# Linear attention and a two-layer FFN on one core: one batch's divisions and x transposition moved ahead of the next batches' loads, and the last group's PSUM tile and stores split

## The chip, the core and the metric

The kernel runs on one core of a Trainium2 chip. The metric is device time in microseconds (us) of one launch. The core has a matrix engine (PE; its weight loads are listed as PEld), a vector engine (DVE), an activation engine (ACT), a general engine (POOL) and an engine that here only issues transfers (SP). Each works through its own instructions strictly in order and waits on semaphores. Transfers are issued from the SP queue, a few from the ACT queue, and are carried out by 16 DMA engines. PE writes its results to PSUM; DVE and ACT move them from there to the on-chip memory (SBUF).

## The reference, cut to what matters

```python
# q, k, v: (8 batches, 8 heads, 576 tokens, 64), float32
theta = pi / 2 * pos / S
phi(x) = concat(relu(x) * cos(theta), relu(x) * sin(theta))      # 64 -> 128 features
kv  = einsum('bhsf,bhsd->bhfd', phi(k), v)
z   = sum over s of phi(k)
num = einsum('bhsf,bhfd->bhsd', phi(q), kv)
den = einsum('bhsf,bhf->bhs', phi(q), z) + 1e-6
x   = (num / den), heads side by side: (4608 tokens, 512)
h   = x @ w_in                     # (4608, 2048)
g   = maximum(0.01 * h, h)
out = g @ w_out                    # (4608, 512), float32
```

## The kernel before, in words

**Groups.** The FFN runs over nine groups of 512 tokens. Group g below 8 is the first 512 tokens of batch g; group 8 collects the last 64 tokens of each of the eight batches. Attention works by batch, and its batch b feeds FFN group b. Batches are counted from 0 here, so that "batch 4" is the fifth.

**Steps of a batch b**, each a small function:
- `load_kv`, `load_main` (lines 124 and 105) issue the loads of k, v and q of the batch, about 1.1 MB each, on SP. They land in `kst`, `vst`, `qst`, tiles of a pool of five.
- `k_cos`, `k_sin` (lines 265 on ACT, 267 on DVE) make phi(k) in `kp`, nine pieces of each; `v_pairs` (line 273 on ACT) casts v into `vm` in two halves; `kv_sum` (line 366) is the 72 short matmuls of kv and z on PE, and ACT casts the result (line 373).
- `q_prep` (line 267, DVE) makes phi(q) of a quarter of the tokens in `qp`, j = 0 to 3; `q_transpose_dma` (line 401) transposes two quarters at a time by DMA from `qp` into `qpT`, issued on SP.
- `num` (line 432) multiplies one quarter with kv on PE, into the only tile of the PSUM pool "n"; `divide` (lines 443 to 448, DVE) divides it into `xs`.
- `x_transpose_dma` (line 413) transposes the batch's `xs` by one DMA into `xT`, issued on SP behind the four divisions.

**The FFN units.** `ffn1(g, m)` is four matmuls with `xT` of the group (line 504); after every second m, ACT applies the leaky ReLU to both (line 512) into `g`. The PSUM pool "h" of these has two tiles, so the activation of one pair of m must be done before the pair after next starts. Groups 1 and 2 use `ffn2` (line 527), sixteen units of four matmuls with `w2`. From group 3 on `ffn2s` uses seven products of half-size blocks instead of eight (line 609): 14 units of eight matmuls of 256 columns. Sums of blocks are made ahead on DVE (`g_sum`, `weight_sum`, line 552), and the products are collected in three PSUM chains, X, Y and Z, from the pool "o" of two tiles; their ends go through DVE (line 552) or ACT (lines 626, 634) to `osb` and are stored from SP (line 659, and in group 8 lines 663 and 650). In group 8 the chain Z is split into two halves, in the pool "h", and these are stored half by SP and half by ACT (line 650).

**What sets the order.** The program is one hand-made list. From group 1 on every FFN unit has a position: group g's units fill the positions 16 g to 16 g + 16, the second layer of group g woven with the first layer of group g + 1. Each attention step is put in with a position of its own, and `weave` issues all steps whose position is at or below a unit's ahead of that unit. A position thus fixes the order on every engine and on the SP queue, not a time. At the place of the change the units stand about 0.46 positions apart (positions 32 to 48, second layer of group 2 and first of group 3) and 0.5 apart from 48 on. The helpers:

```python
out_steps(b, start, step, lag)   # num j at start + j*step; x_transpose at start + 3*step + lag
q_steps(b, start, step, lag)     # q_prep j at start + j*step; q_transpose lag behind j = 1 and 3
kv_steps(b, start, step, mm, eng, on_act, (v0, dv))  # k_cos, k_sin j at start + j*step;
                                 # v_pairs at v0 and v0 + dv; kv_sum at mm
load_steps(b, pk, pv, pq)        # positions of the loads of k, v, q
```

Of the kernel before, what the change touches and what calls it, by code (L numbers as in the profile page):

```python
# [9 lines left out]
dt = mybir.dt  # L10
# [3 lines left out]
P = 128  # L14
J = 4

T = 9
# [3 lines left out]
def kernel(  # L21
# [14 lines left out]
    nc = tc.nc  # L36
# [13 lines left out]
    NG = B + 1  # L50
# [26 lines left out]
    def psum(where, shape, dtype, name):  # L77
        p = {"h": ps_h, "o": ps_o, "n": ps_n}[where]
        return p.tile(shape, dtype, name=name, tag="ps_" + where)

    st = {}
    ACT, DVE, POOL = nc.scalar, nc.vector, nc.gpsimd
# [56 lines left out]
    for i in range(DFF // 512):  # L139
        for c in range(0, NKC, 2):  # L140
            n = 1 if i == 0 and c == 0 else 2
# [42 lines left out]
    def idle(n):  # L184
# [23 lines left out]
        base=0,  # L208
# [3 lines left out]
    for o in range(2):  # L212
# [3 lines left out]
            base=MAIN,  # L216
# [6 lines left out]
            base=0,  # L223
# [315 lines left out]
    NPR, HT, HC = NFT // 2, 2 * P, DM // 2  # L539
# [11 lines left out]
    def tt_op(o, a, b, op):  # L551
        nc.vector.tensor_tensor(out=o, in0=a, in1=b, op=op)  # L552
# [16 lines left out]
    def g_sum(g, n, lo, hi):  # L569
        a11, a12, a21, a22 = (  # L570
            g_quarter(g, r, e, lo, hi) for r in range(2) for e in range(2)
        )
        if n == 1:
            tt_op(S1[:, lo:hi], a21, a22, ALU.add)
        elif n == 2:
            tt_op(S2[:, lo:hi], S1[:, lo:hi], a11, ALU.subtract)
        elif n == 3:
            tt_op(a21, a11, a21, ALU.subtract)
        else:
            tt_op(a12, a12, S2[:, lo:hi], ALU.subtract)  # L580

    def product(g, n):

        return {
            1: (g_quarter(g, 0, 0), w2q[:, 0, 0]),
            2: (g_quarter(g, 0, 1), w2q[:, 1, 0]),
            3: (g_quarter(g, 0, 1), w2q[:, 1, 1]),
            4: (g_quarter(g, 1, 1), T4),
            5: (S1, T1),
            6: (S2, T2),  # L590
            7: (g_quarter(g, 1, 0), w2q[:, 0, 1]),
        }[n]
# [4 lines left out]
    def ffn2s(g, u):  # L597
        n, tt = ORDER7[u // 2], u % 2
        a, b = product(g, n)
        key = "ps7", g, CHAIN[n]  # L600
        apart = g == NG - 1 and CHAIN[n] == "Z"
        if apart:
            key = *key, tt
        first = key not in st
        if first:
            st[key] = psum("h" if apart else "o", [P, 2, HC], dt.float32, "ps_7")
        ps = st[key]
        for i in range(NPR):
            nc.tensor.matmul(  # L609
                ps[:, tt],  # L610
                lhsT=a[:, i, tt * P : (tt + 1) * P],
                rhs=b[:, i],
                start=(first and i == 0),
                stop=(i == NPR - 1 and (apart or tt == 1)),
                skip_group_check=True,
            )
        if apart:
            part = slice(tt * HC, (tt + 1) * HC)
            osb = out_tile(g, HC)
            tt_op(osb, ps[:, tt], {5: t3, 3: t2}[n][:, part], ALU.add)  # L620
            store_tail(2 * (n == 5) + tt, 1, osb)
        if apart or tt == 0:
            return
        flat = ps.rearrange("p t c -> p (t c)")
        if n == 1:
            nc.scalar.copy(t1, flat)
        elif n == 6:
            tt_op(t2, flat, t1, ALU.add)
        elif n == 7:
            tt_op(t3, flat, t1, ALU.add)  # L630
        else:
            osb = out_tile(g, 512)
            if n == 2:
                nc.scalar.copy(osb, flat)
                g_sum(g, 4, 0, NPR)
            else:
                tt_op(osb, flat, {5: t3, 4: t1, 3: t2}[n], ALU.add)
            r, c = {2: (0, 0), 5: (1, 1), 4: (1, 0), 3: (0, 1)}[n]
            store_quarter(g, r, c, osb.rearrange("p (t c) -> p t c", t=2))

    def out_tile(g, n):
        if g == NG - 1:
            return stage.tile([P, n], dt.float32, name="osb", tag="stage")
        return opool.tile([P, n], dt.float32, name="osb", tag="osb")

    def store_tail(tt, c, osb):
        for o in range(2):
            r0 = (2 * tt + o) * S + MAIN
            queue = ACT if o else nc.sync
            queue.dma_start(  # L650
                out[r0 : r0 + TAIL, c * HC : (c + 1) * HC],
                osb[o * TAIL : (o + 1) * TAIL, :],
            )

    def store_quarter(g, r, c, osb):
        cols = slice(c * HC, (c + 1) * HC)
        if g < B:
            rows = out[g * S : g * S + MAIN, :].rearrange("(p j) d -> p j d", j=J)
            nc.sync.dma_start(rows[:, 2 * r : 2 * r + 2, cols], osb)
            return  # L660
        rows = out.rearrange("(t o s) d -> o s t d", o=2, s=S)
        for o in range(2):
            nc.sync.dma_start(
                rows[o, MAIN:S, 2 * r : 2 * r + 2, cols], osb[o * TAIL : (o + 1) * TAIL]
            )

# [103 lines left out]
    def f2(g, i):  # L770
        return lambda: ffn2s(g, i) if g >= G7 else ffn2(g, i)
# [3 lines left out]
    def at(pos, f, *args):  # L775
        steps.append((pos, lambda: f(*args)))
# [96 lines left out]
    def kv_steps(b, start, step, mm, eng_v, on_act=(), vs=None):  # L873
        at(start - 0.01, kp_tile, b)
        for j in range(T):
            at(start + j * step, k_cos, b, j, ACT if j in on_act else DVE)
            at(start + j * step, k_sin, b, j, DVE)
        if vs is None:
            vs = (start + 6 * step, 0.1) if eng_v is DVE else (start + 3 * step, 1)
        v0, dv = vs  # L880
        at(v0, v_pairs, b, 0, 2, eng_v)
        at(v0 + dv, v_pairs, b, 2, 4, eng_v)
        at(mm, kv_sum, b, 0, NC, "n")

    def load_steps(b, pk, pv, pq):
        at(pk, load_kv, "k", k, b)
        at(pv, load_kv, "v", v, b)
        at(pq, load_main, "q", q, b)

    def out_steps(b, start, step, lag):  # L890
        for j in range(J):
            at(start + j * step, num, b, j)
        at(start + (J - 1) * step + lag, x_transpose_dma, b)

    def q_steps(b, start, step, lag):
        for j in range(J):
            at(start + j * step, q_prep, b, j)
            if j % 2:
                at(start + j * step + lag, q_transpose_dma, b, j // 2)
# [17 lines left out]
    load_steps(4, 21.2, 22.5, 21.1)  # L917
    q_steps(4, 30, 0.8, 0.8)
    kv_steps(4, 31, 0.5, 36, ACT)
    out_steps(4, 37.5, 1.9, 1.6)  # L920

    load_steps(5, 31.7, 33.4, 25)
    kv_steps(5, 37.7, 0.75, 46, ACT, range(T), (39.6, 1.2))
    q_steps(5, 38.5, 1.5, 0.6)
    out_steps(5, 49.2, 1.6, 1.2)

    for b in range(6, NG):
        base = 16 * (b - 2)
        if b < B:
            load_steps(b, base - 21, base - 19, base - 22)  # L930
            kv_steps(b, base - 12.5, 0.9, base - 2, ACT, range(T), (base - 9.5, 1.5))
        else:
            for j in range(J):
                at(base - 15 + 2 * j, load_qtail, j)
        q_steps(b, base - 9.5, 1.8, 0.8)
        out_steps(b, base + 1.2, 1.6, 1.2)
# [32 lines left out]
```

## Time and profile before

| | |
|---|---|
| median of 3 runs | 293.45 us (292.05 to 294.54) |
| profiled execution | 293.68 us, its span 291.8 us |
| mean granted PE clock | 0.992 |
| PE busy | 277.4 us, 95% of the span |
| DVE, ACT busy | 166.2 us, 130.5 us |
| HBM read, written | 36.70 MB, 9.44 MB |

The span is from the first to the last instruction of the profiled execution; 1.9 us of its time lie around it. Two views recur. The view of waits lists for an engine which earlier work ended its idle stretches: total us, times, longest. The timeline and the chain of work that ended last start each row with the start and the duration in us from the start of the span; the timeline ends a row with the idle time before it and what ended it, where there was any.

### The profile page before, as it was taken

What the parts mean: (1) busy time and instruction counts of PE and PEld (TensorE: products, weight loads), DVE (VectorE), ACT (ScalarE), POOL (GpSimd) and SP (SyncE); (2) the same over time, 40 slices, a digit from 0 to 9 for tenths busy, and PEclk for the clock granted to TensorE, in tenths of its full rate; (3) what the DMA queues carried; (4) which work ended last, traced back from release to release, by engine and by line L of the source; (5) the groups of instructions that cost most, each with busy time, mean ns of one, the idle gap of its engine ahead of it and who ended that gap; (6) DMA issues with size and microseconds to landing.
All of it is one profiled execution on the core that took longest, in us unless ns stands there. A gap on an engine that the chain in (4) does not pass through costs nothing.

```text
span 291.8 us, 5816 instructions
## 1 busy us (share of the span) xinstructions
PE 277.4 (95%) x2442; PEld 177.9 (61%) x2442; DVE 166.2 (57%) x394; ACT 130.5 (45%) x175; POOL 11.5 (4%) x23
## 2 busy tenths in 40 slices
PE   7899999999999999785999999999999999999993
PEld 3585455555455455443766777777676676667782
DVE  5841597947974936644587458643665524324442
ACT  6856266661065524751485358433324243333300
POOL 2065000000000000000000000000000000000000
PEclk9999999999999999997999999999999999999999
DMA  7999999989999999999059956453296052111123
GB/s 228 336 385 407 387 390 377 142 217 357 194 233 377 303 233 279 273 296 241 13 106 280 250 197 128 98 137 73 77 202 154 2 109 74 36 38 36 46 78 95
DMA packets 78202, 57.53 MB, mean 197 GB/s; under 512 B 50400, under 2 KB 66784, under 8 KB 77792
## 3 DMA queue, kind: packets, MB, share of 16 engines
q1 hardware_dynamic: 77856, 56.89, 72.0%
q8 instruction: 19, 0.31, 0.4%
q10 hardware_dynamic: 320, 0.26, 0.3%
q14 instruction: 7, 0.06, 0.1%
HBM read 36.70 MB, written 9.44 MB: 158 GB/s over the span
## 4 chain that ended last, share of the span: by engine, by line
PE 87%; DMA 6%; ACT 2%; SPq 2%; DVE 1%; issue 1%; DVEq 0%; ACTq 0%
PE ps_h L504 42%; PE ps L609 24%; PE ps_o L527 13%; DMA vst<-in_v_dram 4%; PE ps_kv L366 3%; PE ps_num L432 2%; DMA xT<-xs 2%; SPq L115 1%; ACT g L512 1%; PE ps_xth L484 1%; PE ps_qt L422 1%; SPq L105 1%; PE ps_numh L468 1%; PE ps_idle L187 0%; ACT vm L273 0%
## 5 line engine op out<-in xcount | busy, mean ns | idle before, releaser
L504 PE MATMUL ps_h<-xT,w 128*128 128x512 f16 (+1 forms) x592 | 142.2, 376 | 5.5 <-DMA xT<-xs 3.9
L512 ACT ACTIVATE g<-ps_h 128x1024 f16<-128x1024 f32 x72 | 73.1, 1023 | 95.4 <-PE ps_h L504 95.3
L504 PEld LDWEIGHTS <-w 128*128 128x128 f16 x592 | 65.0, 114 | 48.4 <-DMA xT<-xs 4.4
L609 PEld LDWEIGHTS <-g 128*128 128x128 f16 x480 | 46.5, 98 | 14.2 <-issue 0.2
L609 PE MATMUL ps<-w,g 128*128 128x256 f16 x384 | 48.8, 273 | 0.0
L527 PE MATMUL ps_o<-w,g 128*128 128x512 f16 x192 | 45.0, 379 | 0.0
L527 PEld LDWEIGHTS <-g 128*128 128x128 f16 x192 | 18.2, 98 | 20.0
L609 PE MATMUL ps<-T,ext 128*128 128x256 f16 x192 | 24.6, 273 | 0.5 <-DVE osb L552 0.5
L443 DVE TENSOR_SCALAR den<-ps_num 128x8 f32<-128x8 f32 x28 | 4.6, 166 | 35.6 <-PE ps_num L432 35.4
L609 PEld LDWEIGHTS <-ext 128*128 128x128 f16 x192 | 18.5, 98 | 6.0 <-issue 0.7
L552 DVE TENSOR_TENSOR ext<-g 128x1024 f16<-128x1024 f16 x12 | 8.3, 688 | 21.6 <-ACT g L512 21.6
L552 DVE TENSOR_TENSOR ext<-ps,ext 128x512 f32<-128x512 f32 x12 | 8.3, 692 | 21.5 <-PE ps L609 21.5
L552 DVE TENSOR_TENSOR osb<-ps,ext 128x512 f32<-128x512 f32 (+1 forms) x20 | 12.7, 635 | 13.7 <-PE ps L609 13.6
L448 DVE TENSOR_TENSOR xs<-ps_num,rden 128x512 f16<-128x512 f32 x28 | 19.4, 691 | 1.0
L267 DVE TENSOR_SCALAR kp<-kst,sin_t 128x256 f16<-128x256 f32 x54 | 17.9, 346 | 0.0
L267 DVE TENSOR_SCALAR qp<-qst,cos_t 128x512 f16<-128x512 f32 (+1 forms) x34 | 15.5, 457 | 3.2 <-DMA qst<-in_q_dram 3.2
L265 ACT ACTIVATE kp<-kst,cos_t 128x256 f16<-128x256 f32 (+1 forms) x35 | 15.6, 487 | 0.0
L267 DVE TENSOR_SCALAR qp<-qst,sin_t 128x512 f16<-128x512 f32 (+1 forms) x34 | 15.5, 457 | 0.0
L432 PEld LDWEIGHTS <-qpT 128*128 128x128 f16 (+1 forms) x256 | 10.6, 101 | 5.4 <-issue 1.2
L273 ACT CAST vm<-vst 128x1152 f16<-128x1152 f32 x10 | 11.3, 1147 | 4.1 <-DMA vst<-in_v_dram 4.1
L609 PE MATMUL ps<-ext,g 128*128 128x256 f16 x96 | 12.3, 273 | 0.0
L432 PE MATMUL ps_num<-kv,qpT 128*128 128x66 f16 (+1 forms) x256 | 11.8, 194 | 0.0
(83 smaller groups left out, 182.5 us busy)
## 6 DMA issues: line engine op xcount, KB each, us to landing
out_dram<-osb SPq DMA_DIRECT2D x32, 256.0 KB, 3.0
qst<-in_q_dram SPq DMA_DIRECT2D x7, 1024.0 KB, 8.2
kst<-in_k_dram SPq DMA_DIRECT2D x6, 1152.0 KB, 9.3
vst<-in_v_dram SPq DMA_DIRECT2D x5, 1152.0 KB, 7.5
w2st<-in_moe_w_out_dram SPq DMA_DIRECT2D x3, 1024.0 KB, 12.9
ext<-in_moe_w_in_dram SPq DMA_DIRECT2D x4, 512.0 KB, 10.6
w1st<-in_moe_w_in_dram SPq DMA_DIRECT2D x3, 512.0 KB, 9.4
kst<-in_k_dram SPq DMA_DIRECT2D x2, 576.0 KB, 12.5
```

Of the source, the lines that this page charges most:

```text
L265: nc.scalar.activation(o, i, AF.Relu, scale=col)
L267: eng.tensor_scalar(out=o, in0=i, scalar1=0.0, scalar2=col, op0=ALU.max, op1=ALU.mult)
L273: nc.scalar.copy(o, i)
L366: nc.tensor.matmul(ps[:, o, (c - lo) * NE : (c - lo + 1) * NE], lhsT=st["kp", b][sl, c, j, :], rhs=vm[b % 2][sl, c, j, :], start=(j == 0), ...
L432: nc.tensor.matmul(ps[lo:hi, h // 4, (h % 4) * NE : (h % 4 + 1) * NE], lhsT=qpT[:, h, lo:hi], rhs=kv[b][:, h, :],)
L443: nc.vector.tensor_scalar_add(den.rearrange("p (a b) -> p a b", a=2), ps[:, :, D : 4 * NE : NE], 1e-6)
L448: nc.vector.tensor_tensor(out=xs, in0=ps[:, :, 0 : 4 * NE].rearrange("p a (b e) -> p a b e", e=NE)[:, :, :, 0:D], in1=rden.rearrange("p (a ...
L504: nc.tensor.matmul(ps[:, m % 2, lo:hi], lhsT=w1[m // 4, c][0][:, w1[m // 4, c][1], m % 4 : 512 : 4], rhs=xT[:, lo // P : hi // P, c, :], s ...
L512: nc.scalar.activation(st["g", g][:, m - 1 : m + 1, :], ps, AF.Lrelu)
L527: nc.tensor.matmul(st["ps_o", g, tt], lhsT=st["g", g][:, m, tt * P : (tt + 1) * P], rhs=w2[:, m, :], start=(m == 0), stop=(m == NFT - 1),)
L552: nc.vector.tensor_tensor(out=o, in0=a, in1=b, op=op)
L609: nc.tensor.matmul(ps[:, tt], lhsT=a[:, i, tt * P : (tt + 1) * P], rhs=b[:, i], start=(first and i == 0), stop=(i == NPR - 1 and (apart or ...
```

## The change

It has two parts that do not touch each other.

Around batch 4, in the positions 37 to 60, steps get other positions. Batch 4's divisions (`num` 0 to 3) go from 37.5, 39.4, 41.3, 43.2 to 37.3, 38.7, 40.1, 41.5, and its x transposition from 44.8 to 42.7. For batch 5 the two q transpositions go from 40.6 and 43.6 to 43 and 44.3, both behind batch 4's x transposition now; `k_cos` and `k_sin` go from 37.7 to 43.7 to 39.6 to 44.8, the casts of v from 39.6 and 40.8 to 42.5 and 44, and `q_prep` from 38.5 to 43 to 39 to 43.2. Batch 6's loads go from 42 (q), 43 (k), 45 (v) to 44.6, 45.6, 47, and its `k_cos`, `k_sin` and casts of v start one position later, the former a little closer together. On the SP queue the order

q transposition 5 first half, load q6, load k6, q transposition 5 second half, x transposition 4, load v6, store of group 2's last tile

becomes

x transposition 4, q transposition 5 first half, second half, load q6, load k6, store of group 2's last tile, load v6.

In group 8 the chain Y takes its PSUM tile from the pool "n" (idle by then) and not from "o", and of the two stores of `store_quarter` the second is issued from the ACT queue.

```diff
@@ ffn2s
-            st[key] = psum("h" if apart else "o", [P, 2, HC], dt.float32, "ps_7")
+            where = "n" if g == NG - 1 and key[2] == "Y" else "h" if apart else "o"
+            st[key] = psum(where, [P, 2, HC], dt.float32, "ps_7")
@@ store_quarter
         for o in range(2):
-            nc.sync.dma_start(
+            queue = ACT if o else nc.sync
+            queue.dma_start(
                 rows[o, MAIN:S, 2 * r : 2 * r + 2, cols], osb[o * TAIL : (o + 1) * TAIL]
             )
@@ the list of steps
     load_steps(4, 21.2, 22.5, 21.1)
     q_steps(4, 30, 0.8, 0.8)
     kv_steps(4, 31, 0.5, 36, ACT)
-    out_steps(4, 37.5, 1.9, 1.6)
+    out_steps(4, 37.3, 1.4, 1.2)
 
     load_steps(5, 31.7, 33.4, 25)
-    kv_steps(5, 37.7, 0.75, 46, ACT, range(T), (39.6, 1.2))
-    q_steps(5, 38.5, 1.5, 0.6)
+    for j in range(J):
+        at(39 + 1.4 * j, q_prep, 5, j)
+    for jp in range(2):
+        at(43 + 1.3 * jp, q_transpose_dma, 5, jp)
+    kv_steps(5, 39.6, 0.65, 46, ACT, range(T), (42.5, 1.5))
     out_steps(5, 49.2, 1.6, 1.2)
 
     for b in range(6, NG):
         base = 16 * (b - 2)
+        late = 1 if b == 6 else 0
         if b < B:
-            load_steps(b, base - 21, base - 19, base - 22)
-            kv_steps(b, base - 12.5, 0.9, base - 2, ACT, range(T), (base - 9.5, 1.5))
+            pq, pk, pv = (44.6, 45.6, 47) if late else (base - 22, base - 21, base - 19)
+            load_steps(b, pk, pv, pq)
+            kv_steps(
+                b, base - 12.5 + late, 0.9 - 0.05 * late, base - 2, ACT, range(T),
+                (base - 9.5 + late, 1.5),
+            )
```

## The prediction, on record before the result

> **What bounds the kernel now.** The page gives PE as busy for 95% of the span, so what can be gained is what PE waits for, or work that follows PE's end. The view of waits for PE comes first; its columns are total us, times and longest. Then two stretches of the span by engine; the columns are length, busy us (and count) of PE, PEld, DVE, ACT, POOL, then granted clock, DMA share and GB/s.
>
> ```profile
> PE 277.4 (95%) x2442; PEld 177.9 (61%) x2442; DVE 166.2 (57%) x394; ACT 130.5 (45%) x175; POOL 11.5 (4%) x23
> PE ps_h L504 <- DMA xT<-xs: 3.9, 1, 3.9
> PE ps_h L504 <- ACT g L512: 1.6, 1, 1.6
> PE ps L609 <- DVE osb L552: 0.5, 1, 0.5
> 117.00:124.00 7.00, 5.44 (x40) 2.88 (x39) 4.77 (x15) 5.68 (x9) 0.00 (x0) 1.00 1.05 267
> 124.00:134.40 10.40, 6.48 (x97) 3.48 (x96) 6.03 (x10) 4.26 (x6) 0.00 (x0) 0.97 1.15 253
> ```
>
> The reader is to see that PE's two longest waits each come once, that both lie in 17 us in the middle (7.00 - 5.44 = 1.56 us and 10.40 - 6.48 = 3.92 us idle), and that DMA is busy throughout them. The third wait, 0.5 us, is in the last group's products. The chain of work that ended last, between 108 and 138 us, tells what stands behind the two:
>
> ```profile
> 111.30 6.94 DMA vst<-in_v_dram
> 118.32 1.15 ACT vm L273
> 119.88 0.92 ACT g L512
> 120.84 1.89 PE ps_h L504 x8
> 122.73 0.26 PE ps_num L432 x8
> ...
> 123.85 1.73 PE ps_h L504 x8
> ...
> 127.30 1.25 PE ps_kv L366 x72
> ...
> 129.32 4.95 DMA xT<-xs
> 134.32 3.28 PE ps_h L504 x8
> 137.60 0.87 PE ps L609 x8
> ```
>
> The first wait: ACT works in order, and the cast of batch 5's v sat ahead of an activation (L512) until v landed at 111.30 + 6.94 = 118.24; PE's next pair of units needed that activation's PSUM tile. The second: group 4's first unit needs batch 4's `xT`, transposed by a DMA issued at 129.32 only. The SP queue and DVE say why so late:
>
> ```profile
> 104.86 5.73 SPq L401 DMA_TRANSPOSE qpT<-qp  x1
> 116.13 2.99 SPq L401 DMA_TRANSPOSE qpT<-qp  x1
> 119.79 0.42 SPq L105 DMA_DIRECT2D qst<-in_q_dram  x1
> 120.27 0.70 SPq L124 DMA_DIRECT2D kst<-in_k_dram  x1
> 121.15 8.07 SPq L401 DMA_TRANSPOSE qpT<-qp  x1
> 129.32 2.87 SPq L413 DMA_TRANSPOSE xT<-xs  x1
> 132.29 0.53 SPq L124 DMA_DIRECT2D vst<-in_v_dram  x1
> 123.46 0.69 DVE L448 TENSOR_TENSOR xs<-ps_num,rden 128x512 f16<-128x512 f32 x1
> ```
>
> The last division of batch 4 ended at 123.46 + 0.69 = 124.15, but SP was held from 121.15 to 129.22 in the q transposition issued just behind two loads. A transposition behind fresh loads holds SP for 5.73 or 8.07 us; one without them 2.99 us. The wait also has an echo: the eight matmuls of 512 columns behind it take 3.28 us against 1.73 us elsewhere, so 1.55 us more.
>
> **The change, part by part: the middle.** Three terms can go: 1.56 (activation behind the cast), 3.92 (`xT`), 1.55 (slow matmuls), together 7.03 us. Whether each goes is a matter of placing the new order on times. I count from the row below: a unit of four matmuls takes 1.73 / 2 = 0.865 us, a `num` 0.26 us.
>
> ```profile
> 107.99 1.89 PE L504 MATMUL ps_h<-xT,w 128*128 128x512 f16 x8
> qpT<-qp SPq DMA_TRANSPOSE x1, 9.4
> xT<-xs SPq DMA_TRANSPOSE x7, 5.0
> kst<-in_k_dram SPq DMA_DIRECT2D x6, 1152.0 KB, 9.3
> ```
>
> (Lines two to four end with us from issue to landing; the second is the transposition issued at 104.86.) The 107.99 row is units m = 2 and 3 of group 3. In the new order ten units and three `num` lie between its start and `num` 3, which starts at 107.99 + 10 x 0.865 + 3 x 0.26 = 117.4. In the old trace 1.4 us lie from `num` 3 (122.73) to the end of its division (124.15); so `xs` is done at about 119. On SP the transposition now has only a store ahead of it, and v5, the last load in flight, landed at 118.24. Issued at 119.1 it lands 5.0 us later, at 124.1; with the longest landing above, 9.4, at 128.5. Group 4's first unit is reached at 117.4 + 0.26 + 9 x 0.865 (the rest of the units up to `kv_sum`) + 1.25 (`kv_sum`) + 2 x 0.865 = 128.4. So the `xT` wait goes with 4.3 us to spare, at worst with nothing, and the slow matmuls go with it.
>
> The casts of v5 stand ahead of unit m = 10, so ACT reaches them behind the activation of m = 8 and 9. ACT's pace is read from starts:
>
> ```profile
> 118.32 1.15 ACT L273 CAST vm<-vst 128x1152 f16<-128x1152 f32 x1 [4.13 <-DMA vst<-in_v_dram]
> 119.38 0.51 ACT L265 ACTIVATE kp<-kst,cos_t 128x256 f16<-128x256 f32 x1
> 119.78 1.00 ACT L512 ACTIVATE g<-ps_h 128x1024 f16<-128x1024 f32 x1
> 120.69 0.50 ACT L265 ACTIVATE kp<-kst,cos_t 128x256 f16<-128x256 f32 x1
> ```
>
> A cast takes 1.06 us, a `k_cos` 0.40, an activation 0.91 from start to start. Unit m = 9 ends at 118.55 and its activation starts some 0.2 later, 118.75; one activation and one `k_cos` on, the first cast starts at 120.06. v5 is issued no later than before, so it has been there since 118.24: the 1.56 us go, with 1.8 us to spare.
>
> What is late next? Behind 118.75 ACT has, up to the last `k_cos` of batch 5, three activations, four more `k_cos` and two casts: 3 x 0.91 + 4 x 0.40 + 2 x 1.06 = 6.45, and its own 0.50: it ends at 125.7. `kv_sum` is reached at 125.46 and needs that piece at the 17th of 72 matmuls, 0.28 us on: 125.74. That is even; by whole durations in place of starts ACT would be 0.8 us late. `num` 2 of batch 4 comes at 114.57 and its q transposition landed at 104.86 + 9.4 = 114.26: 0.3 us to spare. DVE has a block of sums that ran inside the old wait:
>
> ```profile
> 130.63 0.69 DVE L552 TENSOR_TENSOR ext<-g 128x1024 f16<-128x1024 f16 x1 [4.29 <-ACT g L512]
> 133.70 0.68 DVE L552 TENSOR_TENSOR g<-g 128x1024 f16<-128x1024 f16 x1
> ```
>
> It takes 134.38 - 130.63 = 3.75 us from the activation of m = 15, which now ends near 128.8; batch 5's first division then starts at 132.6 and ends near 133.7, and the next `num`, which needs its only PSUM tile, comes at 133.9. Three new margins thus lie between 0.0 and 0.3 us. No trace shows them, so I bound their sum: nothing at one end (it can give no gain), 1.56 us at the other, the wait of the same kind above. I take 0, as each count comes out at or above zero.
>
> The moved instructions are the same in number; what pays for the new order is q6 and k6. SP issues three transpositions in a row from 119.1; at 2.99 us each q6 follows at 128.1 and k6 at 128.5, some 8 us later than the 119.79 and 120.27 of before. At 9.3 us k6 lands at 137.8. Its first use stands ahead of unit m = 5 of group 4, at about 128.4 + 9 x 0.865 + 3 x 0.26 = 137.0; but ACT and DVE waiting there delay PE only when the activation of m = 4 and 5 is late for m = 8, some six units later. It would have to land past 141. The load of v6 now stands behind the store of group 2's last tile; that store waits for a copy in DVE's block, near 131, so v6 is issued about when it was (132.29) and its first cast stands ahead of m = 8, near 142. Both cost 0.
>
> **The last group.** Its second product waited for its PSUM tile, until the DVE addition at the end of group 7's chain Z had read it. Here are that wait and the last stores:
>
> ```profile
> 274.77 0.69 DVE L552 TENSOR_TENSOR ext<-ext,g 128x1024 f16<-128x1024 f16 x1
> 275.38 0.68 DVE L552 TENSOR_TENSOR osb<-ps,ext 128x512 f32<-128x512 f32 x1
> 276.12 1.91 PE L609 MATMUL ps<-T,ext 128*128 128x256 f16 x16 [0.55 <-DVE osb L552]
> 285.77 1.29 SPq L663 DMA_DIRECT2D out_dram<-osb  x2
> 286.86 0.42 DVE L552 TENSOR_TENSOR osb<-ps,ext 128x256 f32<-128x256 f32 x1 [0.51 <-PE ps L609]
> 287.16 1.54 SPq L650 DMA_DIRECT2D out_dram<-osb  x2
> ```
>
> PE was free at 276.12 - 0.55 = 275.57. With a tile of pool "n" the product needs only the block sum that ends at 274.77 + 0.69 = 275.46: the whole 0.55 goes, and PE has no wait behind it up to its end, so the end moves by 0.55 too. Behind PE, SP issues the quarter's two stores in 1.29 us (to 287.06), then the last chain's two in 1.54 us (to 288.70). With one quarter store on ACT, SP is free 0.64 us earlier, and the last store is bound by its data, ready at 286.86 + 0.42 = 287.28 instead of an issue start near 288.70 - 0.77 = 287.93: 0.65 us less, at most, and 0 if the transfer of the last bytes and not its issue sets the end. I take 0.58, the earlier end less some 0.07 from data to issue. Both edits: 1.13 us.
>
> The Trainium skill speaks against that edit: "DMA: Bandwidth & Descriptors", section "Rules for kernel authors", says that two transfers of disjoint partition halves serialize on the same 16 engines, whichever queue issues them. By it the sum would lack the 0.58; no row before this change shows it.
>
> **The sum**, against the profiled execution's own time: 293.68 - 7.03 - 1.13 = 285.52 us. The median of the runs, 293.45, lies 0.23 lower, inside their scatter of -1.4 and +1.1 us, and I leave that out: **285.5 us**. A measurement here tells about 1% from no change.
>
> **The rivals.**
> New small waits (12%): ACT's `k_cos`, the `num` or DVE's block come out late by up to 1.56 us: 287.1. For it: three margins of 0.3 us or less. Against: PE has ACT and DVE partly idle in that stretch (5.68 of 7.00 and 4.26 of 10.40 busy on ACT).
> The second store queue brings nothing (10%): 285.5 + 0.58 = 286.1.
> The slow matmuls aren't in the usual run (4%): if their 1.55 us belong to the profiled execution alone, the gain is smaller, 287.1. Against: its time is 0.23 us from the median. The Trainium skill, "TensorE: Matmul & The Clock Gate", Part 1, says that an idle window of about 3.4 us halves the clock and that the window runs free, so that a wait of 3.92 us may or may not be followed by it; this trace agrees as far as it goes, with slow matmuls behind 3.92 us and none behind 1.56.
> The transposition doesn't come first after all (4%): it is held by something on SP that the trace doesn't show, and only the cast's wait and the end are gained: 293.68 - 1.56 - 1.13 = 291.0.
> Slower (5%): the three transpositions in a row hold SP 8.07 us each, as the one behind loads did. Then q6 is issued at 119.1 + 3 x 8.07 = 143.3, k6 lands near 153, and PE stands from about 141 on: 12 us, plus 1.55 us of slow matmuls: 299. With s us each, k6 lands at 119.1 + 3 s + 0.4 + 9.3: PE waits (past 141) from s = 4.1, and the gain of 8.16 is eaten, at 6.6 us of wait and 1.55 of slow matmuls, from s = 6.3. Against: each hold over 5 us in the rows stood behind a load just issued, and here there is none.
>
> **How the numbers follow.** The forecast has 65%; with the first three rivals 91% lie faster by over 1%, 4% within, 5% slower. The range goes from 285.5 less the scatter of 1.4 (284.1) to 285.5 with 1.56 of new waits and the scatter of 1.1 (288.2), rounded outward.
>
> **What would show it.** Right: no wait on `xT<-xs` in PE's list; group 4's first unit near 128.4 with 1.73 us for eight matmuls; the x transposition issued near 119, ahead of q6; ACT's first cast of v5 without a wait; the last group's second product started behind the sum, near 268.5; the last SP issue right behind its data. Wrong: a wait of `kv_sum` on ACT or of L432 on a DMA or DVE, k6 landing past 141, or PE waiting for `kst` through ACT.

## The result, and the profile after

The changed kernel takes 285.07 us (four runs, 285.05 to 285.09), the kernel before 293.73 us in the same comparison (292.05 to 294.54). The ratio is 0.971, with a 95% interval from 0.967 to 0.976. A second comparison on another occasion gave 285.16 against 294.44 us, ratio 0.969 (0.968 to 0.971). The forecast was 285.5. The profiled execution took 285.09 us with a span of 283.3, so 8.59 us less than that of before; the sum said 8.16.

First the page's line for the engines, then the whole list of PE's waits (total us, times, longest), then three stretches in the middle (columns as before: length, busy us of PE, PEld, DVE, ACT, POOL, then clock, DMA share, GB/s).

```profile
PE 275.4 (97%) x2442; PEld 177.7 (63%) x2442; DVE 165.9 (59%) x394; ACT 130.5 (46%) x175; POOL 11.5 (4%) x23
```

```profile
PE ps_idle L187 <- DVE blank L182: 1.2, 1, 1.2
PE ps_qt L422 <- DVE qp L267: 0.9, 1, 0.9
PE ps_numh L468 <- ACT kv L319: 0.7, 1, 0.7
PE ps_kvh L312 <- DVE g L275: 0.2, 1, 0.2
PE ps_xth L484 <- DVE xs L448: 0.2, 1, 0.2
```

```profile
117.00:124.00 7.00, 7.00 (x41) 3.58 (x39) 6.90 (x19) 6.37 (x11) 0.00 (x0) 1.00 0.82 199
124.00:130.40 6.40, 6.40 (x98) 3.73 (x97) 1.62 (x4) 3.18 (x5) 0.00 (x0) 1.00 1.04 225
130.40:165.00 34.60, 34.60 (x339) 24.89 (x337) 22.43 (x51) 18.95 (x27) 0.00 (x0) 1.00 0.92 263
```

All three waits that the prediction started from are off the list; what is left is the start of the kernel. PE is busy through the whole middle, at full clock. The chain shows when each place is reached:

```profile
117.47 0.25 PE ps_num L432 x8
...
125.49 1.25 PE ps_kv L366 x72
...
128.60 1.73 PE ps_h L504 x8
130.32 0.87 PE ps L610 x8
```

Batch 4's last `num` stands at 117.47, `kv_sum` at 125.49, and group 4's first pair of units at 128.60, with 1.73 us for its eight matmuls. The first product behind it starts at 130.32; before, that was 137.60. So the middle gives 7.28 us. What made it possible stands on SP, DVE and ACT, from the timeline:

```profile
118.30 0.69 DVE L448 TENSOR_TENSOR xs<-ps_num,rden 128x512 f16<-128x512 f32 x1
119.06 1.79 SPq L413 DMA_TRANSPOSE xT<-xs  x1
119.94 1.14 ACT L273 CAST vm<-vst 128x1152 f16<-128x1152 f32 x1
120.89 5.19 SPq L401 DMA_TRANSPOSE qpT<-qp  x2
125.05 0.51 ACT L265 ACTIVATE kp<-kst,cos_t 128x256 f16<-128x256 f32 x1
127.05 0.84 SPq L124 DMA_DIRECT2D kst<-in_k_dram  x1
131.27 0.53 SPq L124 DMA_DIRECT2D vst<-in_v_dram  x1
132.50 0.16 DVE L443 TENSOR_SCALAR den<-ps_num 128x8 f32<-128x8 f32 x1
```

The x transposition is issued 0.07 us after the last division's end (118.99), and three transpositions take SP 7 us in all. The cast of v5 has no wait in its row. And the end, again from the timeline:

```profile
267.49 0.69 DVE L552 TENSOR_TENSOR ext<-ext,g 128x1024 f16<-128x1024 f16 x1
268.12 1.91 PE L610 MATMUL ps<-T,ext 128*128 128x256 f16 x16
277.78 0.62 SPq L665 DMA_DIRECT2D out_dram<-osb  x1
277.78 0.66 ACTq L665 DMA_DIRECT2D out_dram<-osb  x1
278.86 0.42 DVE L552 TENSOR_TENSOR osb<-ps,ext 128x256 f32<-128x256 f32 x1 [0.51 <-PE ps L610]
279.31 0.47 SPq L651 DMA_DIRECT2D out_dram<-osb  x1
```

The second product starts without a wait at 268.12, where it stood at 276.12: 8.00 us earlier, 0.72 more than the middle gave. That is more than the idle 0.55 us, because the block of matmuls ahead of it runs on to 268.28 (from 265.50, 2.78 us): without a wait the next block starts 0.16 us before the end that the timeline gives the one ahead, and a wait takes away that overlap too. The last SP issue begins 0.03 us behind its data (279.28).

### The profile page after: what moved, and what is told of

The parts are those of the page before. It is cut to its first block, busy times and chain, and to the rows that moved or that the text cites. A ratio compares the mean times of both kernels' runs of the same rounds, so it can differ in the third digit from the quotient of the medians.

```text
span 283.3 us, 5818 instructions
## 1 busy us (share of the span) xinstructions
PE 275.4 (97%) x2442; PEld 177.7 (63%) x2442; DVE 165.9 (59%) x394; ACT 130.5 (46%) x175; POOL 11.5 (4%) x23
## 4 chain that ended last, share of the span: by engine, by line
PE 93%; DMA 2%; SPq 1%; ACT 1%; DVE 1%; issue 0%; DVEq 0%
PE ps_h L504 44%; PE ps L610 26%; PE ps_o L527 15%; PE ps_kv L366 3%; PE ps_num L432 3%; DMA vst<-in_v_dram 2%; SPq L115 1%; PE ps_xth L484 1%; PE ps_qt L422 1%; SPq L105 1%; PE ps_numh L468 1%; PE ps_idle L187 0%; ACT qpT L273 0%; DVE xT L829 0%; DVE xs L448 0%
```

## The experiments: the middle

The theory is the prediction's: fresh loads ahead of a transposition hold it, and the changed order takes them away. First each half of it alone.

**Only batch 4's divisions and x transposition ahead, batches 5 and 6 as before.**

```diff
 (kernel before)
-    out_steps(4, 37.5, 1.9, 1.6)
+    out_steps(4, 37.3, 1.4, 0.4)      # x transposition at 41.9, loads at 42 and 43
```

> The kernel before with only batch 4's divisions at the new positions and its x transposition at 41.9, ahead of the loads of q6 and k6, which stay at 42 and 43; batches 5 and 6 as before. Theory: the xT wait (3.9 us) and the slow matmuls (1.55 us) go, the 1.6 us for the activation and the old end stay: 293.7 - 5.5 = 288.2 us. The second q transposition of batch 5 is held behind the loads as before, but nothing needs it until the third division: no new wait. Rival (moving the loads back is needed too): PE waits for that q transposition or for the loads, 289 to 292 us.

Measured: 287.25 us (285.78 to 287.88) against 294.67 (ratio 0.976, 0.971 to 0.980), where 288.2 was expected. The wait on `xT` and the slow matmuls are gone. So is, in the profiled execution, the wait for the activation, which was expected to stay. The same middle with the new end was tried next:

> The kernel before with only batch 4's divisions and x transposition moved (transposition at 41.9) and the new end; the steps of batches 5 and 6 stay where they were. Theory: all that is left out against the changed kernel is the place of the casts of v5, whose wait for v5 was 0 to 1.6 us from execution to execution, by when v5 landed: 285.1 + 0 to 1.6, near 286.0 us, with the wait, if any, on an activation and not on a transfer. Rival (the moved loads and transpositions of batches 5 and 6 carry part of the gain): over 287 us.

Measured: 287.06 us against 294.44 (ratio 0.975, 0.973 to 0.977), above the theory's 286.0 and just over the rival's bound. Its profile does show the wait, 1.5 us on the activation, and no wait on a transfer. The landing of v5 tells the two apart. Of the first kernel the issue, from SP's timeline, and then the us from issue to landing, from the transfers issued between 109 and 118 us:

```profile
110.26 0.38 SPq L124 DMA_DIRECT2D vst<-in_v_dram  x1
```

```profile
vst<-in_v_dram SPq DMA_DIRECT2D x1, 1152.0 KB, 6.7
```

and of the second a row of the chain, and one of PE's waits:

```profile
111.77 6.94 DMA vst<-in_v_dram
```

```profile
PE ps_h L504 <- ACT g L512: 1.5, 1, 1.5
```

v5 landed at 116.96 in one and 118.71 in the other, while PE was only 0.2 us later there. The first wait is therefore not a fixed 1.56 us: it is what v5's landing leaves of it in that execution. Two kernels below go the same way: with v5 landing at 117.33 (kernel before with the new end) the wait was 0.7 us, at 117.83 (changed kernel with the casts put back) 1.0.

This kernel is 1.9 us slower than the changed one (285.16 beside it, by the medians). In the two profiled executions (287.61 and 285.01 us) PE comes 2.26 us later to the first product behind group 4's first units (132.51 and 130.25), and nearly all of it has a place: 0.47 stood already at 108 us, ahead of the steps that were moved; 1.45 is the wait; and two pairs of units behind it take 1.89 us to the next start in place of 1.73, together 0.32. Hardly anything is left there for the loads and transpositions of batches 5 and 6, so the rival doesn't hold in this execution, though the median lies at its bound.

**The casts of v5, with `k_cos` and `k_sin`, put back to their old place in the changed kernel.**

```diff
 (changed kernel)
-    kv_steps(5, 39.6, 0.65, 46, ACT, range(T), (42.5, 1.5))
+    kv_steps(5, 37.7, 0.75, 46, ACT, range(T), (39.6, 1.2))
```

> The changed kernel with one thing put back: batch 5's k_cos, k_sin and casts of v at their old positions (casts at 39.6 and 40.8). Theory: the cast again sits ahead of an activation until v5 lands at 118.2, PE waits 1.6 us for the activation, and nothing behind it hides that, since xT now lands 4 us early: 285.1 + 1.6 = 286.7 us, no slow matmuls. Rival (the casts' place is worth nothing by itself, the wait of before was a by-product of the busy queue): 285.1 us.

Measured: 286.11 us (285.71 to 286.58), some 1.0 above the changed kernel and 0.6 below the theory. The changed kernel did not run beside this one; its eight runs, in two other comparisons, lie between 285.01 and 285.30. PE's list has one row more, and the chain names the same cause as before:

```profile
PE ps_h L504 <- ACT g L512: 1.0, 1, 1.0
```

```profile
110.80 7.03 DMA vst<-in_v_dram
117.91 1.15 ACT vm L273
```

So the late casts do pay, by 1.0 us where v5 lands at 117.83. That holds only with the x transposition early, as the next run shows.

**The late casts alone, on the kernel before.** The same `kv_steps` line, the other way round.

> The kernel before with only batch 5's k_cos, k_sin and casts of v at the new positions; the SP order is the old one. Theory by the prediction's sum of terms: the 1.6 us go, 292.1 us. Rival: the two waits lie one behind the other on PE and the second ends at a time set by SP (129.3 + 5.0), not by PE; then the first wait's 1.6 us only move into the second, which grows from 3.9 to about 5.5 us, and the time stays at 293.7 us, with slow matmuls as before or a few more.

Measured: 294.03 against 294.67 us, ratio 0.999 (0.997 to 1.002): nothing. PE's wait on the activation is gone from its list; its wait on `xT` in that list, then the chain, then SP's timeline read:

```profile
PE ps_h L504 <- DMA xT<-xs: 6.4, 1, 6.4
```

```profile
130.40 4.94 DMA xT<-xs
135.38 3.29 PE ps_h L504 x8
```

```profile
121.62 8.68 SPq L401 DMA_TRANSPOSE qpT<-qp  x1
130.40 3.07 SPq L413 DMA_TRANSPOSE xT<-xs  x1
```

The rival holds. PE comes earlier to group 4's first unit (129.0 us, before 130.4) and waits there longer, since `xT` comes when SP is let go. The two waits were never two gains; the first is worth something only once the second is gone.

**What holds a transposition.** Two kernels put loads back ahead of the x transposition in the changed kernel, and one lets it pass the q transposition but not the loads in the kernel before.

```diff
 (changed kernel; only q6 ahead, then q6 and k6)
-            pq, pk, pv = (44.6, 45.6, 47) if late else ...
+            pq, pk, pv = (42, 45.6, 47) if late else ...
+            pq, pk, pv = (42, 42.5, 47) if late else ...
 (kernel before; x transposition at 43.5)
-    out_steps(4, 37.5, 1.9, 1.6)
+    out_steps(4, 37.5, 1.9, 0.3)
```

> The changed kernel with only q6 (1.0 MB) ahead of the x transposition, k6 behind it. Theory (the transposition waits for the bytes ahead of it): q6 alone lands 5 to 7 us after its issue near 118.4, the transposition about 3.3 us behind that as behind q6 and k6 before (129.4 to 132.65), so near 127 to 128.7 and about when PE comes (128.4): 285.1 us, up to 0.5 more. Rival (any fresh load costs the same hold of 8 us and 11.5 us to landing): xT lands near 130.6, 287 to 289 us.

> The changed kernel with the loads of q6 and k6 put ahead of the x transposition again (positions 42 and 42.5, transposition at 42.7). Theory: a transposition behind fresh loads holds SP for about 8 us and lands about 11.5 us after its issue near 119.1, so xT lands near 130.6, PE waits about 2.2 us at group 4's first unit (reached at 128.4), too short for slow matmuls: 287.3 us. Rival (it is only its early issue that counts, loads ahead of it don't hold it): 285.1 us.

> The kernel before with only batch 4's x transposition moved from 44.8 to 43.5, still behind the loads of q6 and k6 and now ahead of the second q transposition of batch 5. Theory (the loads hold whichever transposition comes next): issued at 124.2 when the last division ends, it lands when the loads let it, near 132.7 as that q transposition did; PE waits about 2.3 instead of 3.9 us, which is too short for slow matmuls: 293.7 - 1.6 - 1.55 = 290.5 us. Rival (only the q transposition ahead of it held it, not the loads): it lands at 124.2 + 5.0 = 129.2, no wait: 288.2 us.

Measured: 285.21 us (285.06 to 285.39) with q6 ahead; 289.29 (287.79 to 291.09) with q6 and k6; 291.84 (289.19 to 293.51, ratio to before 0.991, 0.988 to 0.994) with the last. Of the first, SP's timeline and the us from issue to landing of q6 and `xT`:

```profile
118.06 0.43 SPq L105 DMA_DIRECT2D qst<-in_q_dram  x1
118.99 5.61 SPq L413 DMA_TRANSPOSE xT<-xs  x1
```

```profile
qst<-in_q_dram SPq DMA_DIRECT2D x1, 1024.0 KB, 6.8
xT<-xs SPq DMA_TRANSPOSE x1, 7.6
```

Of the second, SP's timeline, the us to landing of k6, the chain and PE's wait:

```profile
118.86 0.70 SPq L124 DMA_DIRECT2D kst<-in_k_dram  x1
119.66 8.59 SPq L413 DMA_TRANSPOSE xT<-xs  x1
```

```profile
kst<-in_k_dram SPq DMA_DIRECT2D x1, 1152.0 KB, 9.6
```

```profile
119.66 12.15 DMA xT<-xs
131.86 3.39 PE ps_h L504 x8
```

```profile
PE ps_h L504 <- DMA xT<-xs: 3.0, 1, 3.0
```

Of the third, PE's wait and the chain:

```profile
PE ps_h L504 <- DMA xT<-xs: 4.3, 1, 4.3
```

```profile
123.30 10.39 DMA xT<-xs
```

The same transposition holds SP for 1.79 us with no load ahead, 5.61 with 1.0 MB and 8.59 with 2.2 MB, and lands at 126.6 and 131.81 in the latter two. In both SP is let go about when the last load ahead lands: at 124.60 with q6 landing at 124.86, and at 128.25 with k6 landing at 128.46. It isn't exact: with only batch 4's steps moved, the q transposition behind q6 and k6 let SP go at 130.31, 1.6 us ahead of k6's landing (131.92). PE comes at 128.5 to 128.9: in the first it waits for nothing, and q6 ahead costs nothing. In the second the wait is 3.0 us, longer than the 2.2 expected, and the slow matmuls, which were expected not to come, came: 285.07 + 3.0 + (3.39 - 1.73) is 289.7, between the median and the profiled execution's 290.02. The last kernel refutes the idea that only the q transposition ahead of it did the harm: issued ahead of that one but behind the loads, the x transposition still takes 10.39 us, and its profiled wait was no shorter than before. The median misses the theory's 290.5 by 1.3 us and the rival's 288.2 by 3.6. The profiled execution, 293.51 us, was the slowest of its kernel; the median is 2.4 us below the kernel before. The last section shows that some runs of this kernel went without the slow matmuls, which accounts for a part of that.

One rival stays open. Loads and transpositions were all issued from SP here, and no run issued these loads from another queue, so it is not shown whether the order of one queue holds the transposition or the 16 DMA engines that all transfers share.

## The experiments: the end

```diff
 (changed kernel: both edits back; only the second back; then the kernel before with both added)
-            where = "n" if g == NG - 1 and key[2] == "Y" else "h" if apart else "o"
-            queue = ACT if o else nc.sync
```

> The changed kernel with the old end: the last group's chain Y in pool o again and both quarter stores on SP. The prediction's terms: 0.55 + 0.58 = 1.13 us slower than the changed kernel, 286.2 us, with PE waiting 0.5 us on the DVE addition. Rival (the end as a whole is set by the landing of the last bytes): 285.6 us, the 0.55 of the tile alone.

> The changed kernel with both quarter stores on SP; the PSUM tile stays new. Theory: the last store's issue starts 0.6 us later, behind the quarter's second one, and the end moves with it: 285.1 + 0.55 = 285.6 us. Rival (two stores share the same 16 DMA engines, so the second queue brings nothing): 285.1 us.

> The kernel before with only the new end (PSUM tile and store queue). Theory: 1.1 us less than before, 292.6 us, inside the scatter of the kernel before; its profile shows the same two waits in the middle, and the scatter of its runs is that of the kernel before (2 us) rather than that of the changed kernel (under 0.1 us), since the waits on transfers are still there.

Measured: 286.32 us (285.96 to 287.49) with the old end, and PE's wait of 0.5 us on the DVE addition is back in its list; 285.73 (285.44 to 285.94) with one store queue alone put back. That is about 0.6 us for each edit (285.73 - 285.1; 286.32 - 285.73), with the changed kernel's 285.1 taken from its own comparisons. On the kernel before both together give 293.27 against 294.24 us, ratio 0.997 (0.995 to 1.000), still with a scatter of 292.4 to 294.1 and with both waits of the middle in its profile (5.2 and 0.7 us). The last issues on SP with one queue read:

```profile
277.85 1.29 SPq L664 DMA_DIRECT2D out_dram<-osb  x2
279.23 1.55 SPq L651 DMA_DIRECT2D out_dram<-osb  x2
```

SP is through at 280.78, against 279.78 in the changed kernel, and the span is 0.6 us longer (283.9 and 283.3). The Trainium skill's rule in "DMA: Bandwidth & Descriptors", section "Rules for kernel authors", that was weighed in the prediction would have made the second queue worth nothing. Here it was worth about 0.6 us, near the 0.62 us that one such issue takes on SP; the Trainium skill leaves it that much on the same page, section "Issuing engines are not separate DMA queues".

## Why the prediction was right, and where it was not

The direction, the size and the places hold. Point by point:

**The xT wait and the slow matmuls** went as said. `num` 3 was placed at 117.4 and came at 117.47; `kv_sum` at 125.46 and came at 125.49; group 4 at 128.4 and came at 128.60. The term is confirmed by the kernel with the transposition alone ahead, and its cause by the holds of 1.79, 5.61 and 8.59 us.

**The activation's wait**, 1.56 us, went, but the step "three terms can go, together 7.03" treats it as a term of its own, and it isn't one: alone it is worth nothing (ratio 0.999), and with `xT` early 1.0 us in the run made for it, and 0 to 1.5 in the three executions with the old place of the casts, by v5's landing. As a sum over both waits the 7.03 is right, since both went. The fourth rival rests on that same step. It gives 291.0 us for the cast's wait and the end without the transposition; by the runs it should have been the end alone, about 292.5.

**The new margins** of 0.0 to 0.3 us held. The last `k_cos` was put at an end of 125.7 and ended at 125.56; DVE's first division of batch 5 was put at 132.6 and stands at 132.50. PE waited for none of them. Taking 0 for their sum was a choice between counts that differed by 0.8 us; the count from starts was the right one here.

**The loads.** q6 and k6 followed the transpositions, 1.5 to 2 us earlier than reckoned (127.05 for k6, reckoned 128.5), as three transpositions took 7 and not 9 us. The 2.99 us were read as the hold without loads, but the transposition at 116.13 had v5 in flight until 118.24; with none in flight the hold is 1.79 us. A wait for k6 did appear, on ACT, and was covered as argued; the transfer's us to landing, and a row of ACT's waits from 132 to 145 us:

```profile
kst<-in_k_dram SPq DMA_DIRECT2D x1, 1152.0 KB, 9.1
```

```profile
ACT kp L265 <- DMA kst<-in_k_dram: 1.2, 1, 1.2
```

k6 landed at 127.05 + 9.1 = 136.2, before the 141 past which, by the prediction's count, PE would have waited. The slower rival did not come; holds of about 8 us were seen only behind 2.2 MB of loads, and here there were none.

**The sum** was 0.43 us short of the profiled difference: the middle gave 7.28 where the idle times and the slow matmuls added up to 7.03, and the end 8.59 - 7.28 = 1.31 where 1.13 was reckoned. Most of it is a term that the sum left out, the overlap that a wait takes away besides the idle time: 0.16 us behind the activation's wait (the pair of units at 120.84 took 1.89 us to the next start, others 1.73) and 0.17 at the end (0.72 - 0.55). Another 0.09 is no gain of the change: PE was that much earlier already at 108 us, ahead of the moved steps. Against the medians more is gained (8.7 and 9.3 us), also because 293.45 was the low side of the kernel before: its later medians are 294.24 to 294.67, and its runs reach 295.80.

**The third rival**, that the slow matmuls aren't in the usual run, did not hold either. The mean granted clock of each run agrees: none of 39 runs of the kernel before for which it is on record is above 0.994, and the changed kernel's eight lie between 0.996 and 1.000.

## What to carry to other kernels

The DMA transposition behind loads just issued was held here until they had landed, or nearly so, and it belongs ahead of them if something is due soon, and the loads can have what slack there is. Waits that lie one behind the other on an engine need not add: ask of each what the next one's end is set by, and count the earlier one only if the later one goes too. Place what has slack by the resource it holds up, not by when it was ready.

## What the runs showed of the hardware that was not expected

**The clock falls after a shorter stop than thought, and not always after the same one.** Two us of the granted clock (the number after the five engines) in the kernel with q6 and k6 ahead, and two of the kernel before:

```profile
131.00:132.00 1.00, 0.14 (x1) 0.14 (x2) 1.00 (x2) 0.00 (x0) 0.00 (x0) 0.74 0.69 152
134.00:135.00 1.00, 1.00 (x4) 0.42 (x3) 0.00 (x0) 0.00 (x0) 0.00 (x0) 0.55 1.12 211
```

```profile
133.00:134.00 1.00, 0.00 (x0) 0.00 (x0) 1.00 (x2) 0.00 (x0) 0.00 (x0) 0.87 1.42 249
137.00:138.00 1.00, 1.00 (x9) 0.62 (x8) 0.00 (x0) 0.30 (x1) 0.00 (x0) 0.93 1.02 405
```

PE stopped at 128.86 in the first and 130.40 in the second. The rows between the two of each kernel read 0.50. Taking a share of 0.74 as half a us at half clock, the fall came about 2.6 us after the stop in one (131.5) and about 3.3 in the other (133.74). The clock was back about 3 us after PE began again in both. Read in the same way, three more kernels give from stop to fall 2.1 us (the one with the x transposition at 43.5), 2.4 (late casts alone) and 5.2 (new end alone), and from PE's next start to the return 4.7, 2.8 and 3.4. So neither delay is fixed. Waits of 1.0 to 1.6 us were not followed by a fall. The Trainium skill, "TensorE: Matmul & The Clock Gate", Part 1, gives an idle window of about 3.4 us, running free; a fall that comes at different delays agrees with the second half of that, but a stop of 3.0 us was enough here, and the fall came as early as 2.1 us after a stop.

**The scatter.** The changed kernel, twice, and the one with q6 ahead ran within 285.01 to 285.39 us in twelve runs. The two with PE waiting for nothing in the middle and an old piece of the end spread over 0.5 and 1.5 us; the kernels that wait for `xT`, the one before among them, over 1.7 to 4.3 us. That the slow matmuls vary from run to run is borne out by the mean granted clock, which is on record for each run. Half clock for 3 us would take some 0.005 off it (0.5 x 3 / 290). Of the ten runs with the x transposition at 43.5, the three fastest, 289.19 to 290.56 us, have 0.999, so the slow matmuls did not come in them; the other seven, 291.34 to 293.51 us, have 0.988 to 0.994. With q6 and k6 ahead the four runs, from fastest to slowest, have 0.996, 1.000, 0.994 and 0.990. How much the waits themselves vary is not shown, as one execution of each kernel was profiled.
